# A transformer-like chain of layers on one Trainium2 core: the last layer's output product written as seven products for eight

## The chip, the cores and the metric

The kernel runs on one core of a Trainium2 chip. The metric is the device time of one execution in microseconds, lower is better. Engines: TensorE (PE in the rows; PEld is its weight load), VectorE (DVE), ScalarE (ACT), GpSimd (POOL) and SyncE (SP), whose queue issues nearly all transfers.

## The reference

Chunked attention over 4 batches, 8 heads and 768 positions gives x, 3072 tokens of 512 features. Two layers follow; the second one is where the change lies:

```python
def _moe_ref(x, w_in, w_out):           # first layer, d_ff 2048
    h = x @ w_in
    g = h * np.cos(h)
    return (g @ w_out).astype(np.float32)

def _moe2_ref(x, w1, w2, w3, w_out):    # second layer, d_ff 768
    h = np.maximum(np.maximum(x @ w1, x @ w2), x @ w3)
    return (h @ w_out).astype(np.float32)
```

## The kernel before, in words

All matrix products are made of three fp32r passes: each operand is split into a high part and a low part (a ScalarE copy that rounds, and a subtraction on VectorE or GpSimd), and high by high, high by low and low by high are accumulated in PSUM (`PASSES`, line 380). One split is a 128x512 tile.

Attention and the first layer fill the first part, in 96 slots (6 blocks of 512 tokens by 16 feature blocks; `slot`, line 878). In a slot TensorE makes 12 matmuls of `p1` and 12 of `p2` two slots earlier, and the helpers make the cosine in between (`chain`, line 424: ScalarE, VectorE, VectorE, ScalarE, VectorE, ScalarE, GpSimd). Beside this, `prep_go` (line 603) decodes and splits the second layer's weights step by step, 1.9 steps per slot on average, and stores them to DRAM: nine steps for each of nine weight groups (`q_steps`), then three for each of six blocks of the output weights (`o_steps`, line 592).

The second layer runs over three pairs of token halves of 512 (`NP`). A pair has nine quads (line 985), then an output stretch (line 1002). A quad (`quad`, line 703) is a 2x2 block product by seven products instead of eight (Strassen's scheme in Winograd's form), over two token halves and two feature halves: 7 products of 6 matmuls into four PSUM banks A, E, F, B. The fifth product accumulates onto bank A, so it follows the ScalarE snapshot of A that the first product left (`snap`, line 714); E and F are used again in the same way. Quads 0, 1, 2 are the three experts w1, w2, w3 of one block of features, 3 to 5 and 6 to 8 the same of the next ones. From the second expert on, VectorE takes running maxima into r11, r12, r22 and r21 as the products end (lines 733 to 748). After the third expert's last product, each maximum is split for the output product: four ScalarE copies, two splits on VectorE and two on GpSimd (lines 755 to 770).

The output stretch (`b_part`, line 789) makes for each of eight blocks of 128 tokens 6 x 3 matmuls, with the split maxima as the stationary operand and the output weights as the moving one, fetched once to SBUF in the first pair and kept. `b_out` copies each bank to SBUF and SP stores it. In the same stretch the next pair's x is combined and split (`x_ops`, line 643): four differences on VectorE, seven pairs of ScalarE copies, splits on GpSimd for B11, T3 and B22 and on VectorE for T1, B21, T2 and T4.

`keep` ties an instruction behind the last one written for its engine, so in quads, operand splits and x operations each engine works in the order of the program text. Weights for the quads are fetched three quads ahead (`fetch`, line 978), as long as 28 buffers allow.

Of the kernel before, what the change touches and what calls it, by code (L numbers as in the profile page):

```python
# [23 lines left out]
S = 768  # L24
# [19 lines left out]
LOOK = 2  # L44
NP, NQ = NB * S // (2 * M), 9
AHEAD = 3
# [31 lines left out]
def attn_moe_kernel(ctx, tc, qT, kT, vw, w_in, w_out, w3, w2o, out):  # L78
# [387 lines left out]
    def p2(j, f):  # L466
        g, w = g_t.pop((j, f)), wA_out[f]
        if f == 0:
            acc[j] = [ps_acc.tile([128, N], F32, tag=f"acc{m}", name=f"acc{m}") for m in range(4)]
        for m in range(4):  # L470
            products(acc[j][m], w, m, [g[:, i, :] for i in range(2 if j or f >= PLAIN else 1)], f == 0, f == FA - 1)
        live[0] -= f >= RES or j == NBLK - 1
        if f == FA - 1:
            for m in range(4):
                if m < 3:
                    t = tr.tile([128, N], F32, tag="r", name="x2")
                elif done[0]:
                    t = tmp["pool"].tile([128, N], F32, tag="ost", name="x2", bufs=2)
# [13 lines left out]
    wd = [[dp.tile([128, 1024 if i < 3 else 512], F32, name=f"wd{q}_{i}") for i in range(4)] for q in range(NQ)]  # L492
    wod = [dp.tile([128, 1024], F32, name=f"wod{f}") for f in range(FB)]

# [16 lines left out]

    def q_pair(q):
        fp, e = divmod(q, 3)
        return ("b", (e, 2 * fp)), ("b", (e, 2 * fp + 1))
# [20 lines left out]
    def q_split(q, i, eng):  # L535
        ev, od = q_parts(q)
        src = (ev[0], ev[1], od[0], od[1][:, :256])[i]
        n = 512 if i < 3 else 256
        store(src, n, eng, wd[q][i])

# [7 lines left out]
    def store(src, n, eng, dst):  # L548
        w = pre.tile([128, 2, n], F32R, tag="p", name="wq")
        keep(ACT.activation(out=w[:, 0, :], in_=src, func=AF.Copy))  # L550
        keep(eng.tensor_tensor(w[:, 1, :], src, w[:, 0, :].bitcast(F32), op=ALU.subtract))  # L551
        later.append((dst, w.rearrange("p a c -> p (a c)").bitcast(F32)))

    def q_fetch(p, q):
        for i in range(4):
            n = 512 if i < 3 else 256
# [34 lines left out]

    def o_steps(f):
        key = ("bo", f)

        def go():
            w_top(key, ACT)
            w_bits(key)
        return [lambda: w_load(key), go, lambda: store(wst.pop(key), 512, DVE, wod[f])]

    prep = [fn for q in range(NQ) for fn in q_steps(q)] + [fn for f in range(FB) for fn in o_steps(f)]  # L600
    prep_n = [0]

    def prep_go(upto):
        while prep_n[0] < min(upto, len(prep)):
            prep[prep_n[0]]()
            prep_n[0] += 1

    def o_fetch(f):
        w = w_tile([128, 2, 512], "wo")
        SP.dma_start(out=w.rearrange("p a c -> p (a c)").bitcast(F32), in_=wod[f])  # L610
        wB_out[f] = (w[:, 0, :], w[:, 1, :])


# [29 lines left out]
    def x_ops(p):  # L643
# [39 lines left out]
        def b21():  # L683
            x_get("B21", u2, DVE)
            live[0] -= 1
        return dict(b11=b11, t1=t1, t3=t3, o3=o3, b21=b21, t2=t2, b22=b22, t4=t4)

# [4 lines left out]
    def product(o, w, half, x, first, last):  # L692
        n = 0
        for c in range(2):
            for a, b in PASSES:
                keep(PE.matmul(o, lhsT=w[:, a, 256 * half + 128 * c:256 * half + 128 * c + 128], rhs=x[c][:, b, :],  # L696
                               start=first and n == 0, stop=n == 5, skip_group_check=True))
                n += 1

    PRODUCTS = (("A", 0, 0, "B11"), ("E", 1, 0, "T1"), ("F", 2, 0, "T3"), ("B", 0, 1, "B21"),  # L700
                ("A", 2, 1, "T2"), ("E", 3, 0, "B22"), ("F", 1, 1, "T4"))

    def quad(p, q):
# [3 lines left out]
        seen = set()  # L707
        t = {}

        def xo(name):  # L710
            t[name] = tmp["pool"].tile([128, M], F32, tag="xo", name=name, bufs=10)
            return t[name]
# [9 lines left out]
        for n, (b, i, half, name) in enumerate(PRODUCTS):  # L722
# [9 lines left out]
            elif n == 3:  # L732
                add(DVE, t["a"], t["a"], bk["B"])
                if e:
                    add(DVE, post["r11"], post["r11"], t["a"], ALU.max)
            elif n == 4:
                snap("u2", "A", True)
                add(POOL, t["p5"], t["p5"], t["u2"])
            elif n == 5:
                t["c12"] = tr.tile([128, M], F32, tag="r", name="c12")  # L740
                add(DVE, t["c12"], t["u2"], bk["E"])
                if e:
                    add(DVE, post["r12"], post["r12"], t["c12"], ALU.max)
                    add(DVE, post["r22"], post["r22"], t["p5"], ALU.max)
            else:
                add(DVE, t["p7"], t["u2"], bk["F"])
                if e:
                    add(DVE, post["r21"], post["r21"], t["p7"], ALU.max)
            yield n
        for i in range(4):  # L750
            wq.pop((p, q, i))
            live[0] -= 1
        if e == 0:
            post.update(r11=t["a"], r12=t["c12"], r21=t["p7"], r22=t["p5"])
        if e == 2:
            for n, (b, i) in enumerate(((0, 0), (1, 0), (1, 1), (0, 1))):
                f = 2 * fp + i
                r = post.pop(("r11", "r12", "r22", "r21")[n])
                k = 4 * fp + n
                if k < 3:  # L760
                    g = gp.tile([128, 2, M], F32R, tag="g", name="g")
                elif k < 7:
                    g = pre.tile([128, 2, M], F32R, tag="p", name="g")
                elif k < 10:
                    g = tmp["pool"].tile([128, 2, M], F32R, tag="g", name="g", bufs=3)
                else:
                    g = w_tile([128, 2, M], "g")
                keep(ACT.activation(out=g[:, 0, :], in_=r, func=AF.Copy))
                keep((POOL if n % 2 else DVE).tensor_tensor(g[:, 1, :], r, g[:, 0, :].bitcast(F32), op=ALU.subtract))
                hB[b, f] = g  # L770

    def b_out(p, o, mt):
        b, m = divmod(mt, M // 128)
        r0 = (2 * p + b) * M + m * 128
        if p == NP - 1 and mt == M // 64 - 1:
            t = w_tile([128, 2, 256], "fin", F32)
            ACT.activation(out=t[:, 0], in_=o[:, :256], func=AF.Copy)
            DVE.tensor_copy(t[:, 1], o[:, 256:])
            SP.dma_start(out=out[r0:r0 + 128, :256], in_=t[:, 0])
            ACT.dma_start(out=out[r0:r0 + 128, 256:], in_=t[:, 1])  # L780
            return
        t = tmp["pool"].tile([128, 512], F32, tag="ost", name="ost", bufs=2)
        if mt % 2 == 0:
            ACT.activation(out=t, in_=o, func=AF.Copy)
        else:
            DVE.tensor_copy(t, o)
        SP.dma_start(out=out[r0:r0 + 128, :], in_=t)

    def b_part(o, mt, fs):
        b, m = divmod(mt, M // 128)  # L790
        for f in fs:
            g, w = hB[b, f], wB_out[f]
            for n, (i, k) in enumerate(PASSES):
                keep(PE.matmul(o, lhsT=g[:, i, 128 * m:128 * m + 128], rhs=w[k],  # L794
                               start=(f == 0 and n == 0), stop=(f == FB - 1 and n == 2)))

# [181 lines left out]
    def fetch(upto):  # L978
        while got[0] <= upto and got[0] < NP * NQ and live[0] + 4 <= NW:
            q_fetch(*divmod(got[0], NQ))  # L980
            got[0] += 1

    rest = [slots[i] for i in range(n2[0], total)]
    for p in range(NP):
        for q in range(NQ):
            for n in quad(p, q):
# [3 lines left out]
                if n == 0:  # L990
                    if p == 0 and 1 < q < 5:
                        o_fetch(2 * q - 4)
                        o_fetch(2 * q - 3)
                    if q == NQ - 2 and p + 1 < NP:
                        x_load(p + 1)
                    fetch(p * NQ + q + AHEAD)
        x_free()
        if p + 1 < NP:
            ops = x_ops(p + 1)
        todo = ["b11", "t1", "t3", "o3", "b21", "t2", "b22", "t4"] if p + 1 < NP else []  # L1000
        os = {}
        for m in range(0, M // 64, 2):
            os.update(zip((m, m + 1), banks(2)))
            if m == 0:
                b_part(os[0], 0, range(4))
                b_part(os[1], 1, range(4))
                b_part(os[0], 0, (4, 5))
                b_part(os[1], 1, (4, 5))
            else:
                b_part(os[m], m, range(6))  # L1010
                b_part(os[m + 1], m + 1, range(6))
            for name in todo[:3]:
                ops[name]()
            todo = todo[3:]
            fetch(p * NQ + NQ - 1 + AHEAD)
            b_out(p, os[m], m)
            b_out(p, os[m + 1], m + 1)
        live[0] -= 2
        hold()
# [4 lines left out]

_OUTS = [((3072, 512), "float32")]

# [49 lines left out]
```

## Time and profile before

| | before |
|---|---|
| median of three runs | 982.78 us (979.46 to 983.20) |
| profiled execution | 984.24 us |
| its span, first to last instruction | 982.4 us |
| TensorE busy | 970.9 us |
| VectorE, ScalarE, GpSimd busy | 554.4, 440.7, 393.4 us |
| mean granted TensorE clock | 0.997 of full |

Busy time of TensorE counts pipelined matmuls, so it is not a measure of how much of its peak is used. The span lies inside the execution's time; the table gives both because durations come from the span and the result is told in the execution's time. Rows of the trace have the form: start, duration, engine, line, operation, output and inputs, shapes, count, and in brackets the idle time before and what ended it.

### The profile page before, as it was taken

How to read it: one execution, taken by the hardware profiler on the slowest of the kernel's cores; microseconds unless marked ns; L12 is line 12 of the kernel's file. 1: busy time of each engine (PE TensorE's matmuls, PEld its weight loads, DVE VectorE, ACT ScalarE, POOL GpSimd, SP SyncE). 2: the span in 40 equal slices, each digit the busy share in tenths (PEclk: the TensorE clock that was granted, in tenths of full speed). 3: DMA queues.
4: the chain of work that ended last, by engine and by line, in shares of the span. 5: the costliest groups of instructions: out<-in, count | busy, mean ns of one | idle time of the engine just before them, and what ended most of it. 6: DMA issues, size and time to landing. Idle time of an engine off the chain costs nothing.

```text
span 982.4 us, 14452 instructions
## 1 busy us (share of the span) xinstructions
PE 970.9 (99%) x5427; PEld 782.8 (80%) x5427; DVE 554.4 (56%) x840; ACT 440.7 (45%) x758; POOL 393.4 (40%) x314
## 2 busy tenths in 40 slices
PE   8999999999999999999999999999999999999998
PEld 5665788878888888888888888888888888888886
DVE  7689656655667566665655564454472455534440
ACT  6667545545445654564445444433242333323320
POOL 3565435534345445444442332343342344324320
PEclk9999899999999999999999999999999999999999
DMA  9986533464557756765487366685715555265001
GB/s 259 348 309 214 178 117 120 146 192 151 195 198 230 235 193 202 202 213 193 166 258 242 127 225 257 213 303 183 231 67 207 190 205 181 76 236 193 32 22 65
DMA packets 67413, 186.01 MB, mean 189 GB/s; under 512 B 7568, under 2 KB 15504, under 8 KB 67344
## 3 DMA queue, kind: packets, MB, share of 16 engines
q1 hardware_dynamic: 67200, 184.96, 56.5%
q8 instruction: 43, 0.70, 0.3%
q14 instruction: 26, 0.21, 0.1%
q10 hardware_dynamic: 144, 0.13, 0.0%
HBM read 140.76 MB, written 44.30 MB: 188 GB/s over the span
## 4 chain that ended last, share of the span: by engine, by line
PE 91%; DVE 3%; DMA 2%; ACT 2%; issue 1%; SPq 0%; POOL 0%; ACTq 0%; DVEq 0%; POOLq 0%
PE hb L696 26%; PE h L392 25%; PE acc L392 22%; PE hb L794 10%; PE s L246 3%; PE s L305 2%; PE acc L389 1%; DMA raw<-in_w2o_dram 1%; DMA pt<-ptd 1%; PE warm L375 1%; DMA raw<-in_w_out_dram 1%; DVE raw L198 1%; PE s L356 0%; ACT top L181 0%; DVE sm L286 0%
## 5 line engine op out<-in xcount | busy, mean ns | idle before, releaser
L392 PE MATMUL h<-x,w 128*128 128x512 f32 x1152 | 286.0, 398 | 0.0
L392 PEld LDWEIGHTS h<-x,w 128*128 128x128 f32 x1152 | 214.7, 189 | 49.3 <-issue 1.4
L462 POOL TENSOR_TENSOR g<-ki,g 128x512 fp32r<-128x512 f32 x80 | 107.9, 1349 | 226.9 <-ACT g L461 195.2
L696 PE MATMUL hb<-x,wq 128*128 128x512 f32 x648 | 155.6, 389 | 0.0
L696 PEld LDWEIGHTS hb<-x,wq 128*128 128x128 f32 x648 | 121.7, 188 | 25.2
L392 PE MATMUL acc<-g,w 128*128 128x512 f32 x576 | 138.5, 389 | 0.0
L392 PEld LDWEIGHTS acc<-g,w 128*128 128x128 f32 x576 | 108.0, 188 | 22.7 <-POOL g L462 0.2
L696 PE MATMUL hb<-xo,wq 128*128 128x512 f32 x486 | 119.1, 389 | 0.0
L392 PE MATMUL acc<-g,wa 128*128 128x512 f32 x480 | 115.7, 389 | 0.1
L696 PEld LDWEIGHTS hb<-xo,wq 128*128 128x128 f32 x486 | 91.2, 188 | 18.9
L392 PEld LDWEIGHTS acc<-g,wa 128*128 128x128 f32 x480 | 90.0, 188 | 19.3 <-POOL g L462 0.5
L455 ACT ACTIVATE ki<-ki,pio 128x512 f32<-128x512 f32 x80 | 57.8, 723 | 101.8 <-DVE ki L453 101.8
L452 DVE SCALAR_TENSOR_TENSOR ki<-h,ki 128x512 f32<-128x512 f32 x80 | 54.9, 687 | 77.8 <-ACT ki L450 75.6
L794 PE MATMUL hb<-wo,g 128*128 128x512 f32 x432 | 98.4, 389 | 0.0
L794 PEld LDWEIGHTS hb<-wo,g 128*128 128x128 f32 x432 | 81.1, 188 | 16.8
L720 POOL TENSOR_TENSOR p<-p,p 128x512 f32<-128x512 f32 x27 | 34.8, 1290 | 130.6 <-ACT p L717 130.6
L457 DVE TENSOR_TENSOR ki<-h,ki 128x512 f32<-128x512 f32 x80 | 55.2, 690 | 54.5 <-ACT ki L455 54.5
L461 ACT ACTIVATE g<-ki 128x512 fp32r<-128x512 f32 x80 | 50.5, 631 | 58.6 <-DVE ki L457 58.4
L450 ACT ACTIVATE ki<-h 128x512 int32<-128x512 f32 x80 | 47.3, 591 | 64.5 <-PE h L392 59.0
L720 DVE TENSOR_TENSOR a<-a,hb 128x512 f32<-128x512 f32 x27 | 18.6, 688 | 93.5 <-PE hb L696 93.5
L198 DVE SCALAR_TENSOR_TENSOR raw<-raw,top 128x512 int32<-128x512 int32 x48 | 46.0, 958 | 14.6 <-ACT top L181 13.9
L551 DVE TENSOR_TENSOR wq<-raw,wq 128x512 fp32r<-128x512 f32 x33 | 39.3, 1204 | 22.2 <-ACT wq L550 22.2
(113 smaller groups left out, 1114.8 us busy)
## 6 DMA issues: line engine op xcount, KB each, us to landing
wq<-wd SPq DMA_DIRECT2D x81, 512.0 KB, 5.0
wa<-wad SPq DMA_DIRECT2D x40, 512.0 KB, 5.8
wd<-wq SPq DMA_DIRECT2D x27, 512.0 KB, 2.9
v<-in_vw_dram SPq DMA_DIRECT2D x24, 384.0 KB, 6.5
raw<-in_w_dram SPq DMA_DIRECT2D x18, 511.8 KB, 5.1
raw<-in_w_in_dram SPq DMA_DIRECT2D x16, 511.8 KB, 10.1
raw<-in_w_out_dram SPq DMA_DIRECT2D x16, 511.8 KB, 10.0
k<-in_kT_dram SPq DMA_DIRECT2D x24, 320.0 KB, 4.6
```

Source lines behind the costliest of these rows:

```text
L198: keep(DVE.scalar_tensor_tensor(o, z, 13, top[key], op0=ALU.logical_shift_right, op1=ALU.bitwise_or))
L392: PE.matmul(o, lhsT=w[a][:, sl], rhs=x[b], start=first and n == 0, stop=last and n == 2)
L450: row(ACT.activation(out=ki, in_=h, func=AF.Copy, scale=INV2PI, bias=0.25))
L452: row(DVE.scalar_tensor_tensor(c, h, INV2PI, ki, op0=ALU.mult, op1=ALU.subtract))
L455: row(ACT.activation(out=c, in_=c, func=AF.Sin, scale=2 * math.pi, bias=pio2))
L457: row(DVE.tensor_tensor(c, h, c, op=ALU.mult))
L461: row(ACT.activation(out=g[:, 0, :], in_=c, func=AF.Copy))
L462: row(POOL.tensor_tensor(g[:, 1, :], c, g[:, 0, :].bitcast(F32), op=ALU.subtract))
L551: keep(eng.tensor_tensor(w[:, 1, :], src, w[:, 0, :].bitcast(F32), op=ALU.subtract))
L696: keep(PE.matmul(o, lhsT=w[:, a, 256 * half + 128 * c:256 * half + 128 * c + 128], rhs=x[c][:, b, :], start=first and n == 0, stop=n == 5, ...
L720: keep(eng.tensor_tensor(o, a, b, op=op))
L794: keep(PE.matmul(o, lhsT=g[:, i, 128 * m:128 * m + 128], rhs=w[k], start=(f == 0 and n == 0), stop=(f == FB - 1 and n == 2)))
```

## The change

The output product becomes seven products for eight as well: over token halves, feature halves and output-column halves. For this the maxima of a pair are combined (r11 becomes r12 - r11, r12 becomes r22 - r12, then r11 becomes r22 less itself and r21 loses the new r11) and seven operands per feature block are split instead of four (`g_oper`): operands 0 to 3 as soon as the third expert's maxima are there, the first two inside the quad, operands 4 to 6 in the output stretch. The output weights are combined and split in the same nine steps as the other weights, three more weight groups (`NG` = 12); they are streamed from DRAM again for each pair, 11 tiles, and are now the stationary operand. The output is written transposed, and the host transposes the result. Two x differences and the one of T3 move from the output stretch into the seventh and eighth quad.

```diff
-NP, NQ = NB * S // (2 * M), 9
+NP, NQ, NG = NB * S // (2 * M), 9, 12
...
+        if isinstance(dst, tuple):
+            c, i = dst
+            for half, n in enumerate(OUT_USE[i]):
+                e = 3 * n + c
+                later.append((wod[e // 2][:, e % 2], w[:, :, 256 * half:256 * half + 256].bitcast(F32)))
+            return
...
     def q_fetch(p, q):
+        if q >= NQ:
+            for i in range(4 * (q - NQ), min(4 * (q - NQ) + 4, 11)):
+                n = 2 if i < 10 else 1
+                w = w_tile([128, n, 2, 256], "wo")
+                SP.dma_start(out=w.bitcast(F32), in_=wod[i][:, :n])
+                wq[p, "out", i] = w
+            return
...
-    prep = [fn for q in range(NQ) for fn in q_steps(q)] + [fn for f in range(FB) for fn in o_steps(f)]
+    prep = [fn for q in range(NG) for fn in q_steps(q)]
...
+        def d1():
+            xs["t1"] = w_tile([128, 2, M], "xt", F32)
+            diff(xs["t1"], v1, u1)
+
+        def d2():
+            xs["t2"] = w_tile([128, 2, M], "xt", F32)
+            diff(xs["t2"], v2, xs["t1"])
+
+        def s1():
+            x_get("T1", xs["t1"], DVE)
+            live[0] -= 2
+
+        def s2():
+            x_get("T2", xs["t2"], DVE)
...
+    OUT_USE = ((0, 3), (1, 6), (2, 4), (5,))
...
             elif n == 3:
                 add(DVE, t["a"], t["a"], bk["B"])
                 if e:
-                    add(DVE, post["r11"], post["r11"], t["a"], ALU.max)
+                    add(DVE, r["r11"], r["r11"], t["a"], ALU.max)
+                    if e == 2:
+                        g_oper(0, fp)
...
-                    add(DVE, post["r12"], post["r12"], t["c12"], ALU.max)
-                    add(DVE, post["r22"], post["r22"], t["p5"], ALU.max)
+                    add(DVE, r["r12"], r["r12"], t["c12"], ALU.max)
+                    add(DVE, r["r22"], r["r22"], t["p5"], ALU.max)
+                    if e == 2:
+                        g_oper(1, fp)
...
+            g_oper(2, fp)
+            g_oper(3, fp)
+            add(POOL, r["r11"], r["r22"], r["r11"], ALU.subtract)
+            add(POOL, r["r21"], r["r21"], r["r11"], ALU.subtract)
...
+    G_SRC = ("r11", "r11", "r12", "r21", "r11", "r22", "r21")
+
+    def g_oper(n, c):
+
+        r = post[c]
+        if n == 1:
+            keep(DVE.tensor_tensor(r["r11"], r["r12"], r["r11"], op=ALU.subtract))
+        elif n == 2:
+            keep(POOL.tensor_tensor(r["r12"], r["r22"], r["r12"], op=ALU.subtract))
+        if n in (0, 4):
+            g = gp.tile([128, 2, M], F32R, tag="g", name="g")
+        elif n in (1, 5):
+            g = pre.tile([128, 2, M], F32R, tag="p", name="g")
+        else:
+            g = w_tile([128, 2, M], "g")
+        src = r[G_SRC[n]]
+        keep(ACT.activation(out=g[:, 0, :], in_=src, func=AF.Copy))
+        keep((POOL if G_POOL[n] else DVE).tensor_tensor(g[:, 1, :], src, g[:, 0, :].bitcast(F32), op=ALU.subtract))
+        hB[n, c] = g
+
+    G_POOL = (1, 0, 1, 0, 1, 0, 0)
+
+    def pair_out(p):
+
+        b = banks(8)
+        bk = [dict(zip("AEFB", b[i::2])) for i in range(2)]
+        seen = set()
+        t = [{}, {}]
+
+        def xo(i, name, pool=None):
+            t[i][name] = (tr.tile([128, M], F32, tag="r", name=name) if pool else
+                          tmp["pool"].tile([128, M], F32, tag="xo", name=name, bufs=6))
+            return t[i][name]
+
+        def snap(i, name, b, pool=None):
+            keep(ACT.activation(out=xo(i, name, pool), in_=bk[i][b], func=AF.Copy))
...
+        for n, (b, _, _, _) in enumerate(PRODUCTS):
+            for i in range(2):
+                for c in range(3):
+                    k, s = divmod(3 * n + c, 2)
+                    w, g = wq[p, "out", k], hB[n, c]
+                    for m, (x, y) in enumerate(PASSES):
+                        keep(PE.matmul(bk[i][b], lhsT=w[:, s, x, 128 * i:128 * i + 128], rhs=g[:, y, :],
+                                       start=b not in seen and c == 0 and m == 0, stop=c == 2 and m == 2, skip_group_check=True))
+            seen.add(b)
+            live[0] -= len([k for k in range(11) if min(2 * k + 1, 20) // 3 == n])
+            live[0] -= 3 * (n in (2, 3, 6))
+            last = p == NP - 1 and n == 6
+            for i in range(2):
+                u = t[i]
+                if n == 0:
+                    snap(i, "a", "A")
+                elif n == 1:
+                    snap(i, "p5", "E")
+                elif n == 2:
+                    snap(i, "p7", "F")
+                    add(POOL, u["p5"], u["p5"], u["p7"])
+                elif n == 3:
+                    add(DVE, u["a"], u["a"], bk[i]["B"])
+                    put(i, 0, 0, u["a"])
+                elif n == 4:
+                    snap(i, "u2", "A", True)
+                    add(POOL, u["p5"], u["p5"], u["u2"])
+                    put(i, 1, 1, u["p5"])
+                elif n == 5:
+                    add(DVE, xo(i, "c12", True), u["u2"], bk[i]["E"])
+                    put(i, 0, 1, u["c12"])
+                elif not last:
+                    add(DVE, u["p7"], u["u2"], bk[i]["F"])
+                    put(i, 1, 0, u["p7"])
...
+    DIFFS = {(NQ - 3, 2): "d1", (NQ - 3, 4): "t3", (NQ - 2, 0): "d2"}
...
+                if p + 1 < NP:
+                    if (q, n) == (NQ - 4, 3):
                         x_load(p + 1)
-                    fetch(p * NQ + q + AHEAD)
+                        ops = x_ops(p + 1)
+                    elif (q, n) in DIFFS:
+                        ops[DIFFS[q, n]]()
...
+        todo = [["b11"], ["s1"], ["o3"], ["b21"], ["s2"], ["b22"], ["t4"]] if p + 1 < NP else []
+        for n in pair_out(p):
+            if n in (1, 2, 3):
+                for c in range(3):
+                    g_oper(3 + n, c)
+            if todo:
+                for name in todo[n]:
+                    ops[name]()
+            fetch(p * NG + NQ + AHEAD + n // 2)
```

The old `b_part`, `b_out`, `o_steps` and `o_fetch` go.

## Rows read from the trace of the kernel before

**Rows 1.** The page: span, TensorE's busy time, and one group (busy, mean ns).

```profile
span 982.4 us, 14452 instructions
...
PE 970.9 (99%) x5427; PEld 782.8 (80%) x5427; DVE 554.4 (56%) x840; ACT 440.7 (45%) x758; POOL 393.4 (40%) x314
...
L551 DVE TENSOR_TENSOR wq<-raw,wq 128x512 fp32r<-128x512 f32 x33 | 39.3, 1204 | 22.2 <-ACT wq L550 22.2
```

**Rows 2.** The chain that ended last: start us, us, what.

```profile
709.59 32.64 PE hb L794 x144
742.23 85.68 PE hb L696 x378
```

**Rows 3.** Waits of TensorE: who for whom, us in total, times, longest.

```profile
PE s L305 <- DMA pt<-ptd: 3.3, 1, 3.3
PE warm L375 <- DVE zero L868: 1.5, 1, 1.5
```

**Rows 4.** Timeline around the end of the first pair's third quad.

```profile
649.22 0.69 DVE L720 TENSOR_TENSOR a<-a 128x512 f32<-128x512 f32 x1
...
650.58 1.29 POOL L720 TENSOR_TENSOR p<-p,u 128x512 f32<-128x512 f32 x1 [1.54 <-ACT u L717]
...
651.22 0.69 DVE L720 TENSOR_TENSOR c<-u,hb 128x512 f32<-128x512 f32 x1 [1.31 <-PE hb L696]
...
652.30 2.88 PE L696 MATMUL hb<-x,wq 128*128 128x512 f32 x12
...
653.37 1.29 POOL L769 TENSOR_TENSOR g<-c,g 128x512 fp32r<-128x512 f32 x1 [1.50 <-ACT g L768]
653.86 1.35 DVE L720 TENSOR_TENSOR p<-p,p 128x512 f32<-128x512 f32 x1
...
655.25 0.63 ACT L768 ACTIVATE g<-p 128x512 fp32r<-128x512 f32 x1 [1.35 <-DVE p L720]
...
655.78 0.58 ACT L717 ACTIVATE a<-hb 128x512 f32<-128x512 f32 x1
655.96 1.61 POOL L769 TENSOR_TENSOR g<-p,g 128x512 fp32r<-128x512 f32 x1 [1.30 <-ACT g L768]
```

**Rows 5.** Timeline early in the first output stretch, VectorE and GpSimd.

```profile
713.46 2.31 DVE L648 TENSOR_TENSOR xt<-xs 128x1024 f32<-128x1024 f32 x1
714.65 2.28 POOL L641 TENSOR_TENSOR x<-xs,x 128x512 fp32r<-128x512 f32 x1
...
716.89 1.74 POOL L641 TENSOR_TENSOR x<-xs,x 128x512 fp32r<-128x512 f32 x1
```

**Rows 6.** Timeline of slots near the end of the first layer.

```profile
581.05 0.58 ACT L450 ACTIVATE ki<-h 128x512 int32<-128x512 f32 x1
...
587.43 0.58 ACT L450 ACTIVATE ki<-h 128x512 int32<-128x512 f32 x1
...
587.93 3.30 PE L392 MATMUL acc<-g,wa 128*128 128x512 f32 x12
...
596.20 0.58 ACT L450 ACTIVATE ki<-h 128x512 int32<-128x512 f32 x1
...
600.15 0.58 ACT L450 ACTIVATE ki<-h 128x512 int32<-128x512 f32 x1
```

**Rows 7.** Busy time of stretches: us, engines, clock, DMA share, GB/s; one transfer.

```profile
742.20:827.90 85.70, 85.70 (x380) 70.99 (x379) 36.47 (x53) 26.17 (x45) 28.94 (x22) 1.00 0.61 211
827.90:860.50 32.60, 32.60 (x146) 27.00 (x145) 20.22 (x21) 11.66 (x21) 13.38 (x8) 1.00 0.22 83
...
wq<-wd SPq DMA_DIRECT2D x81, 512.0 KB, 5.0
```

**Rows 8.** TensorE's longest wait, and the clock behind it (eighth figure).

```profile
99.88 1.97 PE L305 MATMUL s<-pt,v 96*64 96x64 f32 x32 [3.33 <-DMA pt<-ptd]
101.78 5.17 PE L392 MATMUL h<-x,w 128*128 128x512 f32 x12
...
100.00:102.00 2.00, 2.00 (x33) 1.88 (x34) 0.00 (x0) 0.52 (x2) 1.78 (x2) 0.50 0.05 14
...
104.00:106.00 2.00, 2.00 (x6) 1.53 (x5) 0.00 (x0) 0.00 (x0) 0.00 (x0) 0.50 0.84 202
```

More of the change, by code (lines that the diff above doesn't have):

```diff
@@ L477, in p2 @@
                 elif done[0]:
-                    t = tmp["pool"].tile([128, N], F32, tag="ost", name="x2", bufs=2)
+                    t = tmp["pool"].tile([128, N], F32, tag="xo", name="x2", bufs=6)
                 else:
@@ L492, in attn_moe_kernel @@
     wd = [[dp.tile([128, 1024 if i < 3 else 512], F32, name=f"wd{q}_{i}") for i in range(4)] for q in range(NQ)]
-    wod = [dp.tile([128, 1024], F32, name=f"wod{f}") for f in range(FB)]
+    wod = [dp.tile([128, 2, 2, 256], F32, name=f"wod{i}") for i in range(11)]
     def w_tile(shape, name, dtype=F32R):
@@ L512, in q_pair @@
     def q_pair(q):
+        if q >= NQ:
+            return ("bo", 2 * (q - NQ)), ("bo", 2 * (q - NQ) + 1)
         fp, e = divmod(q, 3)
@@ L538, in q_split @@
         n = 512 if i < 3 else 256
-        store(src, n, eng, wd[q][i])
+        store(src, n, eng, wd[q][i] if q < NQ else (q - NQ, i))
     later = []
@@ L551, in store @@
         keep(eng.tensor_tensor(w[:, 1, :], src, w[:, 0, :].bitcast(F32), op=ALU.subtract))
+        if isinstance(dst, tuple):
[4 more added lines that the diff above has]
+            return
         later.append((dst, w.rearrange("p a c -> p (a c)").bitcast(F32)))
     def q_fetch(p, q):
+        if q >= NQ:
+            for i in range(4 * (q - NQ), min(4 * (q - NQ) + 4, 11)):
[4 more added lines that the diff above has]
+            return
         for i in range(4):
@@ L590, in q_steps @@
                 lambda: q_split(q, 2, DVE), end]
[L592 to L598, printed above, removed]
-    prep = [fn for q in range(NQ) for fn in q_steps(q)] + [fn for f in range(FB) for fn in o_steps(f)]
+    prep = [fn for q in range(NG) for fn in q_steps(q)]
     prep_n = [0]
@@ L606, in prep_go @@
             prep_n[0] += 1
[L608 to L611, printed above, removed]
     def x_load(p):
@@ L685, in b21 @@
             live[0] -= 1
-        return dict(b11=b11, t1=t1, t3=t3, o3=o3, b21=b21, t2=t2, b22=b22, t4=t4)
+        def d1():
[9 more added lines that the diff above has]
+            x_get("T2", xs["t2"], DVE)
+        return dict(d1=d1, d2=d2, s1=s1, s2=s2, b11=b11, t1=t1, t3=t3, o3=o3, b21=b21, t2=t2, b22=b22, t4=t4)
     def x_free():
@@ L708, in quad @@
         t = {}
+        r = post.get(fp)
         def xo(name):
-            t[name] = tmp["pool"].tile([128, M], F32, tag="xo", name=name, bufs=10)
+            t[name] = raw_tile(name) if e == 0 else tmp["pool"].tile([128, M], F32, tag="xo", name=name, bufs=6)
             return t[name]
@@ L739, in quad @@
             elif n == 5:
-                t["c12"] = tr.tile([128, M], F32, tag="r", name="c12")
+                t["c12"] = raw_tile("c12") if e == 0 else tr.tile([128, M], F32, tag="r", name="c12")
                 add(DVE, t["c12"], t["u2"], bk["E"])
                 if e:
-                    add(DVE, post["r12"], post["r12"], t["c12"], ALU.max)
-                    add(DVE, post["r22"], post["r22"], t["p5"], ALU.max)
+                    add(DVE, r["r12"], r["r12"], t["c12"], ALU.max)
+                    add(DVE, r["r22"], r["r22"], t["p5"], ALU.max)
+                    if e == 2:
+                        g_oper(1, fp)
             else:
@@ L747, in quad @@
                 if e:
-                    add(DVE, post["r21"], post["r21"], t["p7"], ALU.max)
+                    add(DVE, r["r21"], r["r21"], t["p7"], ALU.max)
+                else:
+                    post[fp] = dict(r11=t["a"], r12=t["c12"], r21=t["p7"], r22=t["p5"])
             yield n
@@ L752, in quad @@
             live[0] -= 1
-        if e == 0:
-            post.update(r11=t["a"], r12=t["c12"], r21=t["p7"], r22=t["p5"])
         if e == 2:
[L756 to L765, printed above, removed]
-                else:
[L767 to L795, printed above, removed]
+            g_oper(2, fp)
+            g_oper(3, fp)
+            add(POOL, r["r11"], r["r22"], r["r11"], ALU.subtract)
+            add(POOL, r["r21"], r["r21"], r["r11"], ALU.subtract)
@@ new lines, in raw_tile @@
+    def raw_tile(name):
+        return tmp["pool"].tile([128, M], F32, tag="raw", name=name, bufs=12)
+    G_SRC = ("r11", "r11", "r12", "r21", "r11", "r22", "r21")
[9 more added lines that the diff above has]
+            g = pre.tile([128, 2, M], F32R, tag="p", name="g")
+        else:
+            g = w_tile([128, 2, M], "g")
[3 more added lines that the diff above has]
+        hB[n, c] = g
@@ new lines, in attn_moe_kernel, with add, put @@
+    G_POOL = (1, 0, 1, 0, 1, 0, 0)
[10 more added lines that the diff above has]
+            keep(ACT.activation(out=xo(i, name, pool), in_=bk[i][b], func=AF.Copy))
+        def add(eng, o, a, b):
+            keep(eng.tensor_tensor(o, a, b, op=ALU.add))
+        def put(i, half, b, src):
+            r0, c0 = 256 * half + 128 * i, (2 * p + b) * M
+            keep(SP.dma_start(out=out[r0:r0 + 128, c0:c0 + M], in_=src))
+        for n, (b, _, _, _) in enumerate(PRODUCTS):
[32 more added lines that the diff above has]
+                    put(i, 1, 0, u["p7"])
+                else:
+                    for h, eng in enumerate((SP, ACT)):
+                        sl = slice(256 * h, 256 * h + 256)
+                        add(DVE, u["p7"][:, sl], u["u2"][:, sl], bk[i]["F"][:, sl])
+                        c0 = 2 * p * M + 256 * h
+                        keep(eng.dma_start(out=out[256 + 128 * i:384 + 128 * i, c0:c0 + 256], in_=u["p7"][:, sl]))
+            yield n
+        for c in range(3):
+            post.pop(c)
@@ L978, in fetch @@
     def fetch(upto):
-        while got[0] <= upto and got[0] < NP * NQ and live[0] + 4 <= NW:
-            q_fetch(*divmod(got[0], NQ))
+        while got[0] <= upto and got[0] < NP * NG and live[0] + 4 <= NW:
+            q_fetch(*divmod(got[0], NG))
             got[0] += 1
+    DIFFS = {(NQ - 3, 2): "d1", (NQ - 3, 4): "t3", (NQ - 2, 0): "d2"}
     rest = [slots[i] for i in range(n2[0], total)]
@@ L990, in attn_moe_kernel @@
                 if n == 0:
[L991 to L994, printed above, removed]
+                    fetch(p * NG + q + AHEAD)
+                if p + 1 < NP:
+                    if (q, n) == (NQ - 4, 3):
                         x_load(p + 1)
-                    fetch(p * NQ + q + AHEAD)
+                        ops = x_ops(p + 1)
+                    elif (q, n) in DIFFS:
+                        ops[DIFFS[q, n]]()
         x_free()
[L998 to L1018, printed above, removed]
+        todo = [["b11"], ["s1"], ["o3"], ["b21"], ["s2"], ["b22"], ["t4"]] if p + 1 < NP else []
+        for n in pair_out(p):
+            if n in (1, 2, 3):
+                for c in range(3):
+                    g_oper(3 + n, c)
[3 more added lines that the diff above has]
+            fetch(p * NG + NQ + AHEAD + n // 2)
         hold()
     tmp_close()
-_OUTS = [((3072, 512), "float32")]
+_OUTS = [((512, 3072), "float32")]
 def kernel(**inputs):
@@ L1061 @@
         ("w3", w3),
-        ("w2o", bits(inputs["moe2_w_out"].reshape(FB, 128, DM))),
+        ("w2o", bits(inputs["moe2_w_out"].reshape(FB // 2, 2, 128, 2, DM // 2).transpose(0, 3, 2, 1, 4).reshape(FB, 128, DM))),
     ]
@@ L1074 @@
     r = run_bass_kernel_spmd(nc, [arrays], core_ids=[0])
-    return r.results[0]["out_0_dram"]
+    return c(r.results[0]["out_0_dram"].T)
```

## The prediction

> **What bounds the kernel now.** I read the page's first part first: TensorE is busy for 970.9 us of the 982.4 us span [rows 1], so the reader looks for what TensorE does and for what it would wait for, and for nothing else. The profiled execution took 984.24 us, 1.84 us around its span; the median of the runs shown is 982.78, 1.46 lower. The chain of waits then shows the last part of the kernel as unbroken matmuls: 32.64 us for the 144 of one output stretch, 85.68 us for the 378 of nine quads [rows 2]. Both give 226.7 ns per matmul, so a matmul of 512 columns has one price, and a quad of 42 costs 9.52 us. The list of waits says that TensorE's longest wait after the start is one of 3.3 us for a transfer [rows 3]; in the part that the change touches it never waits. So time leaves only with matmuls, and comes back with any wait that is new. How near a wait is has to be read from the queues of the helper engines: the timeline around the end of the third quad [rows 4] is the place, because there the splitting of the maxima meets the next quad's first PSUM copy.
>
> **The change part by part.**
>
> *Fewer matmuls.* Before, an output stretch issues 8 x 6 x 3 = 144. After, 7 products x 2 row halves x 3 x 3 passes = 126. 18 fewer in each of three stretches at 226.7 ns [rows 2]: 54 x 0.2267 = 12.2 us less, all of it on the path. Instruction and tile shapes stay, so I take no other price.
>
> *The end of the third, sixth and ninth quad.* Here ScalarE, VectorE and GpSimd get more to do, in a written order. Two facts from rows first. ScalarE works in program order: the first snapshot of the fourth quad, whose product ended near 653.7, starts at 655.78, right behind the copy that had waited for the last maximum [rows 4]. And VectorE and GpSimd hold each other up where VectorE reads two SBUF operands: the maximum of 653.86 meets GpSimd's 653.37 operation (to 654.66), and ends 0.55 us after it, taking 1.35 instead of 0.69; the GpSimd split of 655.96 takes 1.61 instead of 1.29 [rows 4]. Where both have a queue they take turns: GpSimd starts at 714.65 and 716.89 end 1.74 us apart, with one VectorE operation between [rows 5]. VectorE's adds from PSUM (651.22, 0.69 long while GpSimd runs) are not held up.
>
> Now carry the new order along the clock of [rows 4], where the fourth quad starts at 652.30. Until the maximum of r11 ends at 649.91 nothing changes. The copy of r11 (0.63) now stands ahead of the snapshot u2, which ends at 651.1 instead of 650.4. GpSimd splits r11 first (650.65 to 651.94), so its add into p5 moves from 650.58 to 651.94 and ends at 653.23. VectorE's c12 ends at 651.9; its maximum r12 meets that add and ends at 653.8; r22 needs the add's result: 654.4; the new difference r12 - r11: 655.1; its copy: 655.75. GpSimd's new r22 - r12 runs 655.15 to 656.45, the VectorE split behind it ends at 657.0, p7 at 657.65. ScalarE copies r12 by 657.1, GpSimd splits it 657.2 to 658.5, and the last maximum, r21, ends at 659.05 behind that. Its copy takes to 659.7, and only then comes the fourth quad's first snapshot, to 660.2. The quad's fifth product reuses that bank: 24 matmuls after 652.30 is 657.74. Before, the snapshot ended at 656.36, 1.4 us in time; after, TensorE waits 2.4 us. The same order stands at the sixth quad; behind the ninth comes the output stretch, whose fifth product is 16 us away, so there the lateness is absorbed (the second product's last operand is ready 4.7 us in and due at 5.4). Two waits in each of three groups: 6 x 2.4 = 14.4 us. Lower bound, had the two engines never held each other up (each 0.69 and 1.29): the snapshot ends at 658.6, 0.9 us late, 5.4 us in all. Upper bound, one more GpSimd operation of 1.29 let past a waiting maximum: 3.7 each, 22 us. I take 2.4, since the rows show the turns.
>
> The Trainium skill, "SBUF — State Buffer", section "Who interferes with whom", says that a VectorE instruction with two SBUF inputs contends with a GpSimd one that reads SBUF, the first issuer holding the shared pair for its whole length. By that rule the new subtractions on both engines, which no row of before shows, block like the maxima; without it the sum would rest on the lower bound. The trace agrees [rows 4, 5].
>
> *The output stretch.* It now also makes the operands of products five to seven. From the end of the ninth quad GpSimd has 17 two-operand instructions (4 left of the quad, 2 + 2 + 2 for the next x, 3 splits, 4 adds) and VectorE 20 with two SBUF inputs. 17 turns of 1.74 us [rows 5] are 29.6 us, against a stretch of 126 x 0.2267 = 28.6: full. The first wait it gives: VectorE begins with the split of T1 about 12.2 us in, behind ScalarE's backlog; two, three splits for product six, two adds from PSUM, and three splits for product seven make 8 x 1.74 + 1.4 = 15.3, so the last is there at 27.5; it is due at 6 x 4.08 + 1.4 = 25.9: 1.6 late. Behind it stand four more splits, four adds and the difference for T4 (about 8 us, to 35.6); T4's two copies and then the next quad's first snapshot end at 37.2, due at 28.6 + 1.6 + 5.4 = 35.6: again 1.6 late. 3.2 us in each of the two stretches that prepare a next pair, 6.4 us; the third prepares none. Lower bound 0 (the turns overlap more than I think), upper 12 (twice as late). I take 6.4 with the rows that show the turns.
>
> *Preparing the weights.* 18 steps become 27, at the same 1.9 per slot, so they run to slot 92 of 96 instead of 88, beside the preparation of the first x. That stretch is close to a limit: there the chain of one slot starts 6.4 us after the last (581.05 to 587.43) where a free one needs 3.95 (596.20 to 600.15) and a slot has 24 matmuls, 5.44 us, and TensorE already waits 0.4 us at 587.93, a group of 3.30 for 2.88 [rows 6]. Slots 89 to 92 win back 4 x 1.5 = 6 us of lateness now; six ScalarE operations of 0.63 [rows 4] and five on VectorE at the mean 1.20 of a split [rows 1], 9.8 us if all of it stood in the chain, take that back. Bounds 0 and 9.8 - 6 = 3.8; I take 1, for most of it fits beside the chain's own pauses.
>
> *Streamed weights, moved x differences.* 5.25 MB more per pair over about 114 us adds some 46 GB/s to queues that move 211 and 83 GB/s in the two stretches of the second pair [rows 7]; the fetches are issued about two quads (19 us) ahead of use, and one lands in 5.0 us [rows 7]. Nothing queued behind them on SP is due sooner. The three differences moved into quads seven and eight are at most 2.31 each [rows 5], on a VectorE that is busy 43% of the quads [rows 7]. Both 0; if the cover went, one landing per pair, 15 us. The end of the kernel keeps its form: 0.
>
> The sum: -12.2 + 14.4 + 6.4 + 1.0 = +9.6 us. Against the profiled 984.24 that is 993.8, against the median about 992.
>
> **The rivals.**
>
> *The helpers keep up.* For it: both engines idle for half of a pair and more [rows 7]. Against it: the snapshot's margin was 1.4 us and at least 2 us of serial work is put ahead of it. If no wait comes, -12.2 + 1 gives 971.5. It decides if the snapshot ends before 657.74 on that clock. This is the rival on the other side.
>
> *The engines overlap more than in [rows 4].* Six waits of 0.9 us and none in the output: -12.2 + 5.4 + 1 = -5.8, 977. Against it: 653.86 and 655.96.
>
> *The wait costs the clock.* After the one idle stretch of 3.33 us the granted clock read 0.50 between 100 and 106 us, the lower of its levels (1.2 GHz), and the matmuls there took about twice as long [rows 8]: some 3 us more per wait. Six waits of 2.4 us might each do that: up to +18, 1010. Against it: they are shorter, though no row shows how a stretch between 1.5 and 3.3 us ends [rows 3].
>
> *The streamed weights come late.* 15 us on top: 1007. Against it: the share of DMA time, 0.61 and 0.22 [rows 7].
>
> That the change does not do what it says is no rival: the loops fix 126.
>
> **How the numbers follow.** A difference under 0.5% (4.9 us) can't be told from none here. Forecast 0.62, its own range 985 to 999 (waits of 1.5 to 3 us, output waits 0 to 12); all fits 0.12; overlap 0.10; clock 0.12; late weights 0.04. Faster: 0.12 and half of the overlap case, 0.17. Same: the rest of that case and the forecast's low end, 0.11. Slower: 0.72. From 974 to 1003 the range leaves out the rival where all fits and the upper half of the clock and weights cases, 0.2.
>
> **What would show it.** In the waits of TensorE: six new ones for ScalarE's snapshot of bank A, near 2.4 us each, in the fourth and seventh quads; nine quads longer than 85.68 by about 4.8. In the output stretch: 126 matmuls in 28.6 us in the last pair and about 30 in the first two, with a wait for the seventh product's operands, and one in the quad after. VectorE maxima of over 1.2 us at the end of quads three, six, nine. It is wrong if the quads still take 85.68 us, or if the new waits name a transfer, or if the clock falls below 1.00 after them.

## The result, and the profile after

The changed kernel takes 994.44 us (median of six runs, 992.58 to 998.12) where the kernel before takes 981.38 (six runs beside it, 979.46 to 983.20): a ratio of 1.0137, 95% interval 1.0114 to 1.0161, so 13 us slower. Run once more (a0_after below) it gave 994.96 against 981.92, 1.0142 (1.0119 to 1.0165). Ratios and intervals are those on record, over all runs; the two medians alone give 1.0133. Its first profiled execution took 993.47 us, 9.2 above the 984.24 of the one before; the missing 4 us are taken up below, with a0.

The page of the changed kernel, span and busy time, beside [rows 1]: TensorE is busy for 10.5 us less, in a span that is 9.3 us longer.

```profile
span 991.7 us, 14609 instructions
...
PE 960.4 (97%) x5373; PEld 770.2 (78%) x5373; DVE 619.5 (62%) x878; ACT 460.6 (46%) x802; POOL 477.7 (48%) x377
```

The waits of TensorE (who for whom, us in total, times, longest), beside [rows 3]:

```profile
PE hb L712 <- ACT a L735: 16.2, 8, 2.2
PE s L305 <- DMA pt<-ptd: 3.4, 1, 3.4
PE hb L712 <- DVE c L824: 1.5, 2, 0.7
```

L735 is a quad's snapshot, and eight new waits name it: six before the fifth product of a fourth or seventh quad, two in the first quad of the second and third pair. The second line is the wait of [rows 3]. The last one is new as well: VectorE's add at L824 is the output product's c12.

The timeline around the end of the first pair's third quad, beside [rows 4]; the fourth quad starts at 652.32 against 652.30, so the two can be read on one clock:

```profile
651.92 1.29 POOL L738 TENSOR_TENSOR p<-p,u 128x512 f32<-128x512 f32 x1
651.96 1.80 DVE L738 TENSOR_TENSOR c<-c,c 128x512 f32<-128x512 f32 x1
652.32 2.88 PE L712 MATMUL hb<-x,wq 128*128 128x512 f32 x12
...
655.66 1.23 DVE L803 TENSOR_TENSOR g<-a,g 128x512 fp32r<-128x512 f32 x1 [0.70 <-ACT g L802]
...
657.08 1.28 POOL L803 TENSOR_TENSOR g<-c,g 128x512 fp32r<-128x512 f32 x1 [0.74 <-ACT g L802]
657.52 1.39 DVE L738 TENSOR_TENSOR p<-p,p 128x512 f32<-128x512 f32 x1
...
658.94 0.63 ACT L802 ACTIVATE g<-p 128x512 fp32r<-128x512 f32 x1 [1.94 <-DVE p L738]
659.48 0.58 ACT L735 ACTIVATE a<-hb 128x512 f32<-128x512 f32 x1
...
660.11 3.01 PE L712 MATMUL hb<-x,wq 128*128 128x512 f32 x12 [2.19 <-ACT a L735]
```

Read it upwards. TensorE starts the fifth product at 660.11 because the snapshot ends at 660.06; the snapshot stands behind the copy of 658.94; that waited for the maximum of 657.52, which takes 1.39 instead of 0.69 because GpSimd splits an operand from 657.08. The two other VectorE operations that met GpSimd take 1.80 and 1.23. The fifth product was due at 657.76, so TensorE stood for 2.35 us, and the 12 matmuls behind the wait take 0.13 longer than 2.72.

The timeline of the first output stretch and the quad after it, TensorE's rows and the turns of the two helpers:

```profile
714.42 28.94 PE L836 MATMUL hb<-g,wo 128*128 128x512 f32 x126
...
730.11 5.18 DVE L803 TENSOR_TENSOR g<-p,g 128x512 fp32r<-128x512 f32 x3
...
731.29 3.44 POOL L824 TENSOR_TENSOR p<-p,p 128x512 f32<-128x512 f32 x2
...
736.40 4.08 DVE L803 TENSOR_TENSOR g<-p,g 128x512 fp32r<-128x512 f32 x3
...
743.20 2.88 PE L712 MATMUL hb<-x,wq 128*128 128x512 f32 x12
746.82 3.06 PE L712 MATMUL hb<-xo,wq 128*128 128x512 f32 x12 [0.74 <-DVE c L824]
751.41 3.06 PE L712 MATMUL hb<-x,wq 128*128 128x512 f32 x12 [1.54 <-ACT a L735]
```

126 matmuls take 28.78 us from 714.42 to 743.20, against 32.64 for the 144 of [rows 2]. The three VectorE splits of 730.11 take 5.18 us and two GpSimd adds 3.44: turns of 1.72 us, one operation of the engine and one of the other, where [rows 5] has two GpSimd operations that end 1.70 apart (1.74, the prediction's figure, is the length of the second). The three splits of 736.40, for the seventh product, take only 4.08. The quad behind the stretch loses 0.9 us before its third product and 1.9 before its fifth, 2.95 with the slower groups behind the waits.

### The profile page after: what moved, and what is told of

It is laid out like the page before. It is cut to its first block, busy times and chain, and to the rows that moved or that the text cites. A ratio compares the mean times of both kernels' runs of the same rounds, so it can differ in the third digit from the quotient of the medians.

```text
span 991.7 us, 14609 instructions
## 1 busy us (share of the span) xinstructions
PE 960.4 (97%) x5373; PEld 770.2 (78%) x5373; DVE 619.5 (62%) x878; ACT 460.6 (46%) x802; POOL 477.7 (48%) x377
## 4 chain that ended last, share of the span: by engine, by line
PE 74%; DVE 9%; DMA 7%; ACT 4%; POOL 3%; issue 2%; SPq 0%; DVEq 0%; POOLq 0%; ACTq 0%
PE h L392 23%; PE acc L392 22%; PE hb L712 21%; PE hb L836 3%; PE s L246 3%; DMA raw<-in_w_out_dram 2%; PE s L305 2%; DVE p L738 2%; DVE c L738 2%; POOL p L824 1%; DMA raw<-in_w_in_dram 1%; DMA k<-in_kT_dram 1%; ACT g L802 1%; DMA v<-in_vw_dram 1%; DVE g L803 1%
## 5 line engine op out<-in xcount | busy, mean ns | idle before, releaser
L738 POOL TENSOR_TENSOR p<-p,p 128x512 f32<-128x512 f32 x27 | 36.8, 1365 | 105.0 <-ACT p L735 105.0
L836 PE MATMUL hb<-g,wo 128*128 128x512 f32 x378 | 86.6, 390 | 0.0
L836 PEld LDWEIGHTS hb<-g,wo 128*128 128x128 f32 x378 | 70.8, 188 | 15.3 <-DVE g L803 0.6
L450 ACT ACTIVATE ki<-h 128x512 int32<-128x512 f32 x80 | 47.2, 589 | 59.7 <-PE h L392 53.3
L553 DVE TENSOR_TENSOR wq<-raw,wq 128x512 fp32r<-128x512 f32 x36 | 44.1, 1244 | 24.4 <-ACT wq L552 24.4
## 6 DMA issues: line engine op xcount, KB each, us to landing
raw<-in_w_in_dram SPq DMA_DIRECT2D x16, 511.8 KB, 10.3
```

What stands on the lines that cost most here:

```text
L450: row(ACT.activation(out=ki, in_=h, func=AF.Copy, scale=INV2PI, bias=0.25))
L738: keep(eng.tensor_tensor(o, a, b, op=op))
L836: keep(PE.matmul(bk[i][b], lhsT=w[:, s, x, 128 * i:128 * i + 128], rhs=g[:, y, :], start=b not in seen and c == 0 and m == 0, stop=c == 2 ...
```

## The experiments

**e1: does GpSimd's turn lengthen the wait?** The two engines' meeting is tried alone here. GpSimd's split of operand 2 is no link in ScalarE's order: nothing but the sharing with VectorE ties it to the snapshot.

```diff
         if e == 2:
-            g_oper(2, fp)
+            low = g_oper(2, fp, fp < 2)
             g_oper(3, fp)
+            if fp < 2:
+                pending.append(low)
+                pending.append(subs)
```

`pending` is worked off in the next quad behind its third snapshot; `low` is the split, `subs` the two GpSimd subtractions.

> Only GpSimd's split of operand 2 and its two subtractions at the end of quads three and six move behind the next quad's third snapshot; every ScalarE and VectorE instruction keeps its place. Theory (VectorE and GpSimd take turns on two-SBUF operations, so the maximum of r21 stands behind that split): the maximum falls from 1.39 to about 0.7 us, and each of the six waits before the fifth product from about 2.3 to 1.6 us, some 4 us in all: about 990. Rival (the waits come from the program order on ScalarE alone, where this split has no part): the six waits stay at 2.2 to 2.35 us and the time at 994.

Measured: 988.87 us, ratio to the kernel before 1.0079 (1.0064 to 1.0094). In its timeline the maximum and the wait are:

```profile
656.61 0.69 DVE L740 TENSOR_TENSOR p<-p,p 128x512 f32<-128x512 f32 x1
...
658.50 3.02 PE L712 MATMUL hb<-x,wq 128*128 128x512 f32 x12 [1.49 <-ACT a L737]
```

The maximum fell from 1.39 to 0.69 and each of the six waits from 2.19 to 1.49 (the bracketed idle time): the 0.70 us that this one meeting cost, six times over. The rival, order alone, falls. The Trainium skill, "SBUF — State Buffer", "Who interferes with whom", has this rule (two SBUF inputs on VectorE contend with a GpSimd instruction that reads SBUF), and the trace agrees, with 0.69 against 1.39.

**e2: is it what stands ahead of the snapshot?** Everything that operands 2 and 3 of the first two blocks need goes behind the next quad's third snapshot; their tiles are still taken at the old place.

```diff
         if e == 2:
-            g_oper(2, fp)
-            g_oper(3, fp)
-            add(POOL, r["r11"], r["r22"], r["r11"], ALU.subtract)
-            add(POOL, r["r21"], r["r21"], r["r11"], ALU.subtract)
+            if fp < 2:
+                pending.append(rest)
+            else:
+                rest()
```

> Operands 2 and 3 of blocks one and two (differences, ScalarE copies, splits) are made behind the next quad's third snapshot instead of ahead of its first. Theory (ScalarE reaches the snapshot too late): the six waits of 2.35 us in quads four and seven vanish, quads take 85.7 us per pair plus the 2.8 at the start of pairs two and three; 14 to 15 us less, about 980. Rival (the lateness only moves on): waits of a like size appear at the operands of products three and four or in the quads after, and the time stays above 988.

Measured: 976.52 us, ratio 0.9952 (0.9937 to 0.9966). The waits of TensorE that are left in the changed part:

```profile
PE hb L712 <- ACT a L737: 3.1, 2, 1.6
PE hb L712 <- DVE c L837: 1.5, 2, 0.8
```

The six are gone, and no other took their place, so the whole of each wait came from what the order puts ahead of the snapshot. This alone makes the kernel faster than before. The time fell by 18 us where 14 to 15 were expected; from the first quad to the end of the span the profile is 15.0 us shorter than the changed kernel's, as the waits say, and the rest lies ahead of the quads.

**e3: the other four waits.** The order of the next x changes, and nothing else.

```diff
+                if p and (q, n) == (0, 2):
+                    ops["t4"]()
...
-        todo = [["b11"], ["s1"], ["o3"], ["b21"], ["s2"], ["b22"], ["t4"]] if p + 1 < NP else []
+        todo = [["b11", "s1"], [], ["o3"], ["b21"], [], ["s2"], ["b22"]] if p + 1 < NP else []
```

> Only the order of the next x in the output stretch changes: T1 is split right behind B11, T2 and B22 behind the last PSUM adds of the sixth and seventh product, T4 in the next quad behind its third snapshot. Theory (VectorE and GpSimd are full in that stretch, so what stands last is late): the two waits of 0.9 and 1.9 us in the first quad of pairs two and three vanish, 5.5 us less, about 989; the six other waits stay at 2.35. Rival (these waits come from the streamed weights or the lateness of quads): they stay.

Measured: 986.32 us, ratio 1.0052 (1.0036 to 1.0069). The wait for c12 and two of the eight for the snapshot are gone from its list; six stay:

```profile
PE hb L712 <- ACT a L735: 13.1, 6, 2.2
```

Both effects are as expected. The time fell by 8 us where the waits account for 6; in the profiled executions of e2 and e3 the quads also begin at 615.9 and 615.6 us instead of 618.3, before anything that was edited, and that start differs from run to run.

**e4: both.** The edits of e2 and e3 together.

> Both moves together. Theory: no wait of TensorE is left from quads on, the saving of 54 matmuls is what remains, 12 us below the kernel before: about 970, ratio about 0.988. Rival (prepared weights, streamed weights or the longer tail cost something of their own that the waits hid): 973 to 980.

Measured: 971.01 us (970.39 to 973.15) against 981.52, ratio 0.9900 (0.9884 to 0.9915). From the quads on TensorE waits for nothing, and the three output stretches stand in its timeline as

```profile
708.19 28.72 PE L849 MATMUL hb<-g,wo 128*128 128x512 f32 x126
...
822.43 28.76 PE L849 MATMUL hb<-g,wo 128*128 128x512 f32 x126
...
936.71 28.72 PE L849 MATMUL hb<-g,wo 128*128 128x512 f32 x126
```

114.2 us from one to the next, which is 504 matmuls (378 and 126) at 226.7 ns. From the first quad to the end of the span that makes 352.1 us against 364.1 in the profile of before: the seven products keep 12.0 of the 12.2 us that they save, once their operands are not in the way. By the medians it is 10.5; the missing 1.5 us may lie ahead of the quads, where the start differs from run to run, but what costs them is not shown. This version beats both kernels.

**e5: is the streaming hidden?** On e4, each streamed tile is fetched twice.

```diff
-                SP.dma_start(out=w.bitcast(F32), in_=wod[i][:, :n])
+                for _ in range(2):
+                    SP.dma_start(out=w.bitcast(F32), in_=wod[i][:, :n])
```

> On the version with both moves, each tile of the streamed output weights is fetched twice into the same place, so 5.25 MB more per pair. Theory (the streaming is hidden): no new wait of TensorE, 971 as without. Rival (the streaming costs transfers that the quads need): waits for a transfer appear, or the time rises by 3 us or more.

Measured: 974.28 us, ratio 0.9929 (0.9906 to 0.9953), 3 us above e4, with a wait that names the transfer:

```profile
PE hb L850 <- DMA wo<-wod: 2.0, 2, 1.3
```

The rival's sign is there, but the edit does more than double the bytes. The second fetch writes the tile that the first one writes, and SP's queue stands before it until the first has landed. In the waits of SP's queue:

```profile
SPq L568 <- DMA wo<-wod: 125.9, 33, 4.7
```

That is one wait for each of the 33 tiles. The fetches for the first output stretch, in e4 and then in e5:

```profile
679.83 25.27 SPq L567 DMA_DIRECT2D wo<-wod  x11
```

```profile
680.53 52.66 SPq L568 DMA_DIRECT2D wo<-wod  x22
```

The last tile's first copy landed at 732.86 and its second, issued behind that landing, at 736.04; TensorE, which was due to read the tile at 734.74, went on at 736.17. So the lateness comes from this chain of waits, and e5 does not tell whether twice the bytes would be hidden. That the streaming as written is hidden shows without it: in the changed kernel and in e4 no matmul waits for `wo`, and in their traces every tile is issued at least 22.9 us, and landed at least 19.7 us, before the first matmul that reads it.

**a0 and the missing 4 us.** The changed kernel again, unedited.

> The changed kernel as it is, beside the kernel before once more. Theory (its waits and 54 fewer matmuls are all there is, plus 9.3 us in the profiled execution): about 991 where before is 981.5, ratio near 1.0095; the further 3 to 4 us in the first six runs were the spread of the start, which reads its inputs at the transfers' full rate. Rival (something in every run but the profiled one costs 3 to 4 us more): ratio 1.0137 again, 994.5.

Measured: 994.96 us, ratio 1.0142 (1.0119 to 1.0165). My reading, that the further 3 to 4 us were the spread of the start, fell. The second profile has the same ten waits, but two of them cost more. Its timeline at the third pair's fourth and seventh quads, and the busy time of stretches there (the granted clock is the eighth figure):

```profile
904.64 4.59 PE L712 MATMUL hb<-x,wq 128*128 128x512 f32 x12 [2.17 <-ACT a L735]
...
937.26 4.23 PE L712 MATMUL hb<-x,wq 128*128 128x512 f32 x12 [2.19 <-ACT a L735]
941.29 1.97 PE L712 MATMUL hb<-xo,wq 128*128 128x512 f32 x6
```

```profile
904.60:907.00 2.40, 2.36 (x6) 1.88 (x7) 1.11 (x2) 0.97 (x2) 1.74 (x2) 0.51 0.27 109
...
909.00:911.00 2.00, 2.00 (x11) 1.65 (x10) 0.99 (x2) 0.00 (x0) 0.64 (x1) 1.00 0.81 256
```

Behind the first of the two the granted clock was 0.51, so the lower level of 1.2 GHz, and 12 matmuls took 4.4 us (904.64 to 909.07) where they took 2.85 to 2.9 behind the others; behind the second it fell as well, and the slow matmuls reach into the next group (1.97 us for six, elsewhere 1.52). Such a fall costs 1.6 us in all: the third pair's nine quads take 96.80 us (865.35 to 962.15) and the second pair's, with the same waits, 93.61. In the first profile none of the waits did that. The mean clock of single runs fits: 992.58 us at 0.997, 995.86 at 0.993, 998.12 at 0.991.

**e6 and e7: the clock.** If the wait's length decides how often the clock falls, longer waits must show it. ScalarE's copy of r21 is done twice (e6) or three times (e7).

```diff
-        keep(ACT.activation(out=g[:, 0, :], in_=src, func=AF.Copy))
+        for _ in range(2 if n == 3 and c < 2 else 1):
+            keep(ACT.activation(out=g[:, 0, :], in_=src, func=AF.Copy))
```

> On the changed kernel, the ScalarE copy of r21 is done twice in a row at the end of quads three and six, one more instruction of about 0.53 us ahead of the snapshot: each of the six waits grows from 2.35 to about 2.9 us. Both theories: 3.2 us more from the waits themselves, 998. Theory (a wait of this length sometimes takes the granted clock down for a few us, as two of eight did in the second profile of the changed kernel): longer waits do it more often, so the mean clock falls below the 0.995 of the changed kernel's runs, and the time passes 999. Rival (the clock's falls have nothing to do with these waits): mean clock 0.995 as before, 998 or less.

> The same with the copy done three times: waits of about 3.4 us, as long as the one of 3.3 to 3.5 in the first layer, behind which the profiles shown have the clock at half. 6.4 us more from the waits: 1001. Theory: most of the six waits now halve the clock for some 3 to 6 us, up to 3 us more each, mean clock 0.985 or less and the time 1008 to 1018. Rival: mean clock 0.995, 1001.

Measured: e6 1003.48 us, ratio 1.0215 (1.0197 to 1.0234), mean clocks 0.990 and 0.991; e7 1008.31 us, 1.0264 (1.0242 to 1.0287), 0.986 to 0.992. Three of e6's waits:

```profile
658.78 4.39 PE L712 MATMUL hb<-x,wq 128*128 128x512 f32 x12 [2.85 <-ACT a L735]
692.09 3.01 PE L712 MATMUL hb<-x,wq 128*128 128x512 f32 x12 [2.84 <-ACT a L735]
...
909.32 4.58 PE L712 MATMUL hb<-x,wq 128*128 128x512 f32 x12 [2.83 <-ACT a L735]
```

and two of e7's:

```profile
659.55 4.59 PE L712 MATMUL hb<-x,wq 128*128 128x512 f32 x12 [3.50 <-ACT a L735]
...
821.72 3.04 PE L712 MATMUL hb<-x,wq 128*128 128x512 f32 x12 [3.50 <-ACT a L735]
```

A group behind a wait takes either about 3.0 or 4.2 to 4.6 us, so each wait can be counted. Of six waits in a profile, the slow kind followed 0 of 6 at 1.49 us (e1), 0, 2 and 0 of 6 at 2.19 (the changed kernel twice, and e3), 4 of 6 at 2.85 and 5 of 6 at 3.50. e6's time grew by 8.5 us where its waits alone grew by 6 x 0.65 = 3.9, e7's by 13.4 where they grew by 7.9. The profiles close the sum: from the first quad to the end of the span e6 is 10.3 us longer than the first profile of the changed kernel, which is 3.9 and four falls of 1.6, and e7 15.9, which is 7.9 and five falls of 1.6. e7's mean clock did not come down to the 0.985 expected, since a fall costs 1.6 us and not 3. That these waits take the clock down, and more often the longer they are, is shown. Length is not all of it: in the first layer the clock fell behind the wait for `pt` in all ten profiles, also in e3, where that wait was shorter than 2.2 us and stood before matmuls of another shape (granted clock 0.51 from 99.8 to 103.3 us):

```profile
98.59 1.15 PE L305 MATMUL s<-pt,v 96*64 96x64 f32 x32 [1.97 <-DMA pt<-ptd]
99.67 4.61 PE L392 MATMUL h<-x,w 128*128 128x512 f32 x12
```

What decides whether a given wait does it is open.

## Why the prediction was right

The side, the place and the size hold: 992 was predicted and 994.4 measured, in the likeliest case's own range. The main term, six waits for one snapshot, is right in mechanism and in size; that the whole sum comes within 0.4 us of the difference of the first two profiles is luck, since two smaller terms were wrong and the clock came on top. By its steps:

*Fewer matmuls*, -12.2: the stretches take 28.78, 28.78 and 28.57 us of TensorE's time, 11.8 less in all; the 0.2 us above 28.57 in each of the first two belongs to the output stretch below.

*End of the third, sixth and ninth quad*, +14.4: six waits of 2.35 us and some 0.15 for the slower group behind each, 15.0. The hand-carried clock put the snapshot's end at 660.2, and it is 660.06; the three VectorE operations that it had behind GpSimd are the three long ones. The lower bound of 0.9 (no sharing) is excluded by e1. The ninth quad costs nothing, as said.

*The output stretch*, +6.4: 6.3 (2 x 2.95 and 2 x 0.2), but the working was half wrong. The wait for the seventh product's operands was put at 1.6 and is at most the 0.2: VectorE began with T1's split 12.4 us in (12.2 was said), but the last operand was there 26.1 us in and not 27.5, since not every split cost a full turn. In its place there is one that I did not see: 0.9 us before the next quad's third product, whose bank is still held by the output's c12. The step counted the turns up to each operand and let VectorE's adds from PSUM follow at no one's cost; but what stands behind them is a bank. The snapshot's wait was put at 1.6 and is 1.9. That 6.3 meets 6.4 is chance.

*Preparing the weights*, +1.0: 0. From the ScalarE copy at 197.60 (L450) to the first quad it is 420.7 us, against 420.8 from the same copy before, and 420.7 in the other eight profiles; TensorE is busy for 131.82 of the 132 us from 480 to 612 (131.92 before). The added steps did fit beside the chain's pauses. The spread of the start, with first quads from 615.6 to 618.3 us, lies before that copy.

*Streamed weights and moved differences*, 0: 0, with no wait for `wo` and each tile landed 19.7 us or more ahead of its use. The added rate is 48 GB/s and not 46 (21 slots of 256 KB are 5.5 million bytes, in 114 us), which changes nothing; where the cover would end is not shown.

*The end*, 0: TensorE's last group ends 3.8 us before the span's end, against 3.5.

*The clock* was a rival at 0.12 and up to 18 us. It is neither of the cases as I priced them: it comes with some waits, at 1.6 us each and not 3. The prediction named a clock below 1.00 after the waits as a sign of being wrong; none of the first profile's six had it, two of six in a0's did, so by its own sign this part was missing from the sum. The other steps sum to -12.2 + 15.0 + 6.3 + 0.3 = 9.4 us, the difference of the first two profiles, and a0's two falls make 12.6 of it. Its runs have a median mean clock of 0.995 where the runs of before beside them have 0.998, and 0.003 of 990 us is 3 us, which fits. In the first six runs the median clock is 0.997, so there the falls explain less; the profiled execution of before was also 2.9 us above its median. One to two of the 13 us may lie ahead of the quads, as in e4; their cause stays open.

## What to carry to other kernels

Where one engine is busy all the time, price a change by the order that it writes for the others: carry the queues forward by hand to the first instruction that the busy engine needs, and let a VectorE operation with two SBUF inputs and a GpSimd operation follow each other, not overlap. Work whose result is due later goes behind the copy that frees a bank, not ahead of it: here that placement alone (e2) turned 1.4% slower into 0.5% faster, and with the new order of the next x (e4) 1.0%. And a wait of TensorE can cost more than its length.

## What was not expected

The clock fell behind waits of 2.2 us in two cases of eighteen, where the trace of before had shown only one of 3.33 us [rows 8]; a fall cost 1.6 us, about half of the 3 us that I had read from [rows 8]. A test that fetches each tile twice into the same place tests the order of a queue and not its rate: e5's tile came 1.3 us late while the DMA engines were busy for only 0.60 of that stretch (709 to 737 us, 213 GB/s). And the first 12 matmuls behind the waits of the quads took 0.13 to 0.18 us longer even with the clock at 1.00.
